# First weights in two transfers: rows 0 to 15, then rows 16 to 127

## The chip, the cores and the metric

The kernel runs on one core of a Trainium2 chip. It is one launch, and all inputs lie in the chip's memory when it starts. The metric is the device time in microseconds (us); lower is better. All data are 32-bit floats.

The core has five engines that run side by side and wait for each other by semaphores: TensorE (matmuls), VectorE, ScalarE, GpSimd, and SyncE, which computes nothing and here issues the transfers. Sixteen DMA engines move the bytes. On-chip memory has 128 rows (partitions); a transfer names a stretch of each row that it fills.

## The reference, cut to what matters

One token goes through a transformer block with adaptive layer norm. Attention has 32 heads of width 192 and a cache of 8192 positions, and an MLP with squared ReLU follows.

```
mod = silu(c) @ w_mod                        # (640) @ (640, 3840): sa, ca, ga, sb, cb, gb
h = layernorm(x) * (1 + ca) + sa
q = h @ wq                                   # (640) @ (640, 6144)
p = softmax(q . k_cache / sqrt(192))         # 32 heads x 8192 positions
x = x + ga * ((p . v_cache) @ wo)
h = layernorm(x) * (1 + cb) + sb
x = x + gb * (relu(h @ w1 + b1) ** 2 @ w2 + b2)
```

The two caches are 201 MB each. Nearly all that is moved is read once and used once.

## The kernel before, in words

**Layout and slots.** The host lays every input out so that a transfer reads one long contiguous stretch for each of the 128 rows. On chip there are three large slots, which are reused in turn (`slot`). The first holds the first weights (`wm0_t`); the chunks of the caches follow in the next ones. `PLAN` lists the chunks; each holds some key positions, some units of values, and now and then a block of `wq` or `wo`. After the chunks come three more loads: the rest of `w_mod`, then `w1`, then `w2`.

**The first weights.** `wm0` has 128 rows of 8514 floats (34,056 bytes a row, 4257 KB in all): the columns of `w_mod` for `sa` and `ca` except for a part of their last block of rows, the first block of `wq`, and x, c and the biases. One transfer brings it (L131). The rest of that last block comes as `wm0x` in six small transfers (L134), by the table `XP`. Its entries are (first row, rows, slabs): the rows of one such transfer lie four apart, as 32, 36, ..., 60 or 0, 4, 8. The place that they fill is set to zero first, half of it by VectorE (L129) and half by GpSimd (L130), so SyncE waits for these two before it issues L134.

**The order of the work at the start.** SyncE issues, in program order: the first weights (L131), the six small transfers (L134), the first and second chunk (L249, `load(0)` and `load(1)`), and the third chunk (`load(2)`) once the first slot has been used up. From then on it issues chunk n + 3 when chunk n has been used up. On the compute side VectorE copies x, c and the biases out of the first weights (L138), ScalarE and VectorE make silu(c) (L186 to L189), TensorE multiplies by the columns of `w_mod` (L207, L213), the layer norm follows (L166 to L181), then the first block of queries (L266). Only then can VectorE multiply the first keys (L285).

**The steady part.** For each chunk, VectorE multiplies keys by the query (L285) and sums each product over the width (L293), with a share of the sums done by GpSimd (L411). TensorE takes the values (L334). The order is written out by hand (`manual_schedule`), and the framework adds the semaphores: a reader waits for the transfer that fills its tile, and a transfer into a slot waits for the slot's last readers.

**The end.** The six transfers of `w2` each have a semaphore of their own. `finish` multiplies each part as it lands (L491), VectorE adds up (L499 to L502), and two small transfers write the result.

Of the kernel before, what the change touches and what calls it, by code (L numbers as in the profile page):

```python
# [13 lines left out]
P = 128  # L14
# [26 lines left out]
SX = 7  # L41
XP = ((32, 8, 5), (0, 3, SX), (1, 3, SX), (2, 3, SX), (3, 3, 6), (33, 1, SX))
WX = 3 * DG
W0 = KB * 2 * D - WX
VPC = 5
LEAD_FROM = 1300
# [54 lines left out]
def block_kernel(ctx: ExitStack, tc: tile.TileContext, kept, kv, wm0, wm0x, wm1, w1, w2):  # L101
    nc = tc.nc
# [7 lines left out]
    def slot(name):  # L110
        taken.append(name)
        return kept["slots"][(len(taken) - 1) % 3]
# [14 lines left out]
    wm0_t = slot("wm0_t")  # L127
    wm0x_t = wm0_t[:64, SLOT - SX * WX:]
    nc.vector.memset(wm0x_t[:, :SX // 2 * WX], 0.0)  # L129
    nc.gpsimd.memset(wm0x_t[:, SX // 2 * WX:], 0.0)  # L130
    nc.sync.dma_start(wm0_t[:, :wm0.shape[1]], wm0)  # L131
    r = 0
    for a, k, n in XP:
        nc.sync.dma_start(wm0x_t[a:a + 4 * k:4, :n * WX], wm0x[r:r + k, :n * WX])  # L134
        r += k

    small = const.tile([P, 2 * KB + SX + FB + KB], F32, name="small")
    nc.vector.tensor_copy(small, wm0_t[:, W0 + WQ:wm0.shape[1]])  # L138
    x_c, c_c, bbc = small[:, :KB], small[:, KB:2 * KB + SX], small[:, 2 * KB + SX:]
# [122 lines left out]
    def query(u, w):  # L262
        w = w.rearrange("p (b n) -> p b n", b=KB)
        ps = psum.tile([P, 512], F32, tag="q", name=f"ps_q{u}", bufs=2)
        for b in range(KB):
            nc.tensor.matmul(ps, h1[:, b:b + 1].to_broadcast([P, P]), w[:, b], start=(b == 0), stop=(b == KB - 1))  # L266
        nc.scalar.activation(qb[:, QC * u % RING:QC * u % RING + QC], ps, AF.Copy, scale=DH ** -0.5)  # L267
# [4 lines left out]
    nc.gpsimd.memset(att_s, 0.0)  # L272
    query(0, wm0_t[:, W0:W0 + WQ])

# [295 lines left out]
```

## Time and profile before

| | |
|---|---|
| time, median of 3 runs | 1050.31 us (1050.29 to 1050.44) |
| the profiled execution's own time | 1050.39 us |
| its span, first to last instruction | 1049.1 us |
| bytes read from the chip's memory | 451.82 MB |
| mean rate over the span | 431 GB/s |
| VectorE busy | 826.6 us (79%) |
| TensorE busy | 490.4 us (47%) |
| GpSimd busy | 190.4 us (18%) |
| ScalarE busy | 44.9 us (4%) |

Times in the trace count from the span's start. A group's line has its source line, engine, operation, tiles (written <- read) and shapes, then its count, busy time and mean length, then the idle time of the engine before it and what ended most of that. In the table of stages a packet of a transfer counts in the stage in which it starts. [...]

### The profile page before, as it was taken

What the parts mean: (1) busy time and instruction counts of PE and PEld (TensorE: products, weight loads), DVE (VectorE), ACT (ScalarE), POOL (GpSimd) and SP (SyncE); (2) the same over time, 40 slices, a digit from 0 to 9 for tenths busy, and PEclk for the clock granted to TensorE, in tenths of its full rate; (3) what the DMA queues carried; (4) which work ended last, traced back from release to release, by engine and by line L of the source; (5) the groups of instructions that cost most, each with busy time, mean ns of one, the idle gap of its engine ahead of it and who ended that gap; (6) DMA issues with size and microseconds to landing.
All of it is one profiled execution on the core that took longest, in us unless ns stands there. A gap on an engine that the chain in (4) does not pass through costs nothing.

```text
span 1049.1 us, 5218 instructions
## 1 busy us (share of the span) xinstructions
PE 490.4 (47%) x2162; PEld 136.0 (13%) x2162; DVE 826.6 (79%) x407; ACT 44.9 (4%) x122; POOL 190.4 (18%) x61
## 2 busy tenths in 40 slices
PE   3253334455352363436254366344445336436288
PEld 1010011111010010101011011011111002001023
DVE  1799878886959969888697895999887977988912
ACT  0100000000000000000000000000000000000001
POOL 1113121121212211212121121122221211311300
PEclk9676576777675686668766576676776767768689
DMA  9999999999999999999999999999999999999998
GB/s 408 431 434 433 432 433 435 437 434 436 438 437 434 431 433 431 433 433 434 432 436 435 435 435 432 433 429 435 431 438 438 434 438 434 433 435 431 421 425 364
DMA packets 9433, 452.16 MB, mean 431 GB/s; under 512 B 1065, under 2 KB 1325, under 8 KB 1709
## 3 DMA queue, kind: packets, MB, share of 16 engines
q1 hardware_dynamic: 9406, 451.83, 99.6%
q8 instruction: 17, 0.28, 0.1%
q14 instruction: 6, 0.05, 0.0%
q10 hardware_dynamic: 4, 0.00, 0.0%
HBM read 451.82 MB, written 0.00 MB: 431 GB/s over the span
## 4 chain that ended last, share of the span: by engine, by line
DMA 54%; DVE 33%; PE 12%; ACT 1%; issue 0%; SPq 0%; DVEq 0%; ACTq 0%
DMA slot<-in_kv 50%; DVE slot L285 17%; DVE sc L293 13%; PE ps_o L334 6%; DMA slot<-in_w 3%; PE ps_q L266 2%; PE att_a L366 2%; DMA slot<-in_wm 1%; DVE os L348 1%; PE ps_mx L309 1%; DVE om L346 1%; ACT p L317 0%; PE ps_mod L207 0%; PE att_a L368 0%; PE ps_mod L213 0%
## 5 line engine op out<-in xcount | busy, mean ns | idle before, releaser
L285 DVE TENSOR_TENSOR slot<-slot,qb 128x8064 f32<-128x8064 f32 (+19 forms) x81 | 419.7, 5211 | 127.0 <-DMA slot<-in_kv 121.9
L293 DVE TENSOR_REDUCE sc<-slot 128x25 f32<-128x4800 f32 (+21 forms) x109 | 333.9, 3096 | 0.4
L411 POOL TENSOR_TENSOR slot<-slot 128x1824 f32<-128x1824 f32 (+9 forms) x51 | 187.3, 3673 | 801.2 <-DVE slot L285 698.3
L334 PE MATMUL ps_o<-slot,p 128*32 128x512 f32 x1536 | 291.5, 725 | 70.4 <-DMA slot<-in_kv 60.9
L309 PE MATMUL ps_mx<-ident,mp 128*128 128x128 f32 x32 | 14.5, 452 | 347.9 <-DVE mp L307 347.9
L334 PEld LDWEIGHTS ps_o<-slot,p 128*32 128x32 f32 x1536 | 68.0, 130 | 269.8 <-issue 200.4
L366 PE MATMUL att_a<-slot,oW 128*32 128x512 f32 x96 | 64.8, 831 | 44.9 <-ACT oW L364 44.9
L266 PE MATMUL ps_q<-slot,ln_h 128*128 128x512 f32 x120 | 71.8, 759 | 26.9 <-DMA slot<-in_kv 24.7
L309 PEld LDWEIGHTS ps_mx<-ident,mp 128*128 128x128 f32 x32 | 5.6, 176 | 375.9 <-DVE mp L307 307.6
L317 ACT ACTIVATE p<-sc,nm 128x256 f32<-128x256 f32 x32 | 16.2, 507 | 650.4 <-DVE nm L311 650.4
L266 PEld LDWEIGHTS ps_q<-slot,ln_h 128*128 128x128 f32 x120 | 28.8, 251 | 67.2 <-issue 36.9
L346 DVE TENSOR_TENSOR om<-ps_o,mask 96x512 f32<-96x512 f32 x32 | 21.6, 675 | 8.9 <-PE ps_o L334 8.9
L311 DVE TENSOR_REDUCE nm<-ps_mx 128x1 f32<-128x128 f32 x32 | 9.3, 292 | 19.6 <-PE ps_mx L309 19.6
L366 PEld LDWEIGHTS att_a<-slot,oW 128*32 128x32 f32 x96 | 12.2, 142 | 81.2 <-ACT oW L364 47.6
L348 DVE TENSOR_REDUCE os<-om 96x64 f32<-96x512 f32 x32 | 21.8, 682 | 1.1
L356 DVE TENSOR_REDUCE oT<-ps_oT 128x3 f32<-128x96 f32 x16 | 4.0, 248 | 20.4 <-PE ps_oT L352 20.4
L322 PE MATMUL ps_sum<-ident,wide 128*128 128x128 f32 x16 | 7.5, 466 | 22.4 <-ACT wide L320 22.4
L352 PE MATMUL ps_oT<-ident,os 96*128 96x96 f32 x16 | 5.0, 313 | 25.4 <-DVE os L348 25.3
L207 PE MATMUL ps_mod<-slot,silu 128*32 128x480 f32 (+2 forms) x78 | 9.2, 610 | 14.4 <-DVE silu L189 14.4
L368 PE MATMUL att_a<-slot,oW 128*96 128x384 f32 x32 | 14.2, 524 | 0.0
L364 ACT ACTIVATE oW<-oT,r 128x96 f32<-128x96 f32 x16 | 5.9, 372 | 174.4 <-DVE oT L356 174.4
L267 ACT ACTIVATE qb<-ps_q 128x512 f32<-128x512 f32 x12 | 7.2, 597 | 131.9 <-PE ps_q L266 131.9
(81 smaller groups left out, 91.4 us busy)
## 6 DMA issues: line engine op xcount, KB each, us to landing
slot<-in_kv SPq DMA_DIRECT2D x38, 8064.0 KB, 35.4
slot<-in_kv SPq DMA_DIRECT2D x11, 8000.0 KB, 37.4
slot<-in_kv SPq DMA_DIRECT2D x2, 7872.0 KB
slot<-in_kv SPq DMA_DIRECT2D x1, 6144.0 KB, 22.8
slot<-in_wm SPq DMA_DIRECT2D x1, 4480.0 KB
slot<-in_wm SPq DMA_DIRECT2D x1, 4257.0 KB, 12.5
slot<-in_kv SPq DMA_DIRECT2D x1, 3264.0 KB
slot<-in_kv SPq DMA_DIRECT2D x1, 3072.0 KB
```

Source lines behind the costliest of these rows:

```text
L266: nc.tensor.matmul(ps, h1[:, b:b + 1].to_broadcast([P, P]), w[:, b], start=(b == 0), stop=(b == KB - 1))
L285: nc.vector.tensor_mul(pr, pr, q[:, None, :].to_broadcast([P, b - a, DH]))
L293: nc.vector.tensor_reduce(sc[:, a % SRING:a % SRING + b - a], src[:, a - first:b - first], axis=AX.X, op=ALU.add)
L309: nc.tensor.transpose(ps[:, :P], mp.to_broadcast([P, P]), ident)
L311: nc.vector.tensor_reduce(nm, ps[:, :P], axis=AX.X, op=ALU.max, negate=True)
L317: nc.scalar.activation(p, s[:, :, None].to_broadcast([P, NPOS, 32 // E]), AF.Exp, bias=nm, accum_out=sp[:, h % 2:h % 2 + 1])
L334: nc.tensor.matmul(ps_t[h][32 * g:32 * (g + 1)], p[:, E * j:E * (j + 1)].rearrange("p e r -> p (e r)"), t[:, g], start=(j == 0), stop=last)
L346: nc.vector.tensor_mul(om[:n], ps_t.pop(h)[:n].rearrange("p (d e) -> p d e", e=E), mask[:n, None, :].to_broadcast([n, ED, E]))
L348: nc.vector.tensor_reduce(os_[:n, h % 2], om[:n], axis=AX.X, op=ALU.add)
L366: nc.tensor.matmul(att_a[96:, :512], oW[:, j], w[:, j, :512], start=(first and j == 0), stop=(last and j == NV - 1))
L368: nc.tensor.matmul(att_a[:96, :NV * (D - 512)], oW.rearrange("p j r -> p (j r)"), w[:, :, 512:], start=first, stop=last)
L411: nc.gpsimd.tensor_add(half, half, kt[:, m:, DH // 2:])
```

## The change

The transfer of the first weights is split by rows. SyncE first issues rows 0 to 15, in full width, and then rows 16 to 127, in full width. The bytes, their source and their place are the same. The transfers of L134 and of the chunks follow in the same order as before. Readers of the first weights wait for both transfers. The split uses a new constant, 16.

```
@@ -41,6 +41,7 @@
 WX = 3 * DG
+FIRST = 16
 W0 = KB * 2 * D - WX
@@ -128,7 +129,8 @@
     nc.vector.memset(wm0x_t[:, :SX // 2 * WX], 0.0)
     nc.gpsimd.memset(wm0x_t[:, SX // 2 * WX:], 0.0)
-    nc.sync.dma_start(wm0_t[:, :wm0.shape[1]], wm0)
+    for a, b in ((0, FIRST), (FIRST, P)):
+        nc.sync.dma_start(wm0_t[a:b, :wm0.shape[1]], wm0[a:b])
     r = 0
     for a, k, n in XP:
         nc.sync.dma_start(wm0x_t[a:a + 4 * k:4, :n * WX], wm0x[r:r + k, :n * WX])
```

More of the change, by code (lines that the diff above doesn't have):

```diff
@@ L43 @@
 WX = 3 * DG
+FIRST = 16
 W0 = KB * 2 * D - WX
@@ L130, in block_kernel @@
     nc.gpsimd.memset(wm0x_t[:, SX // 2 * WX:], 0.0)
-    nc.sync.dma_start(wm0_t[:, :wm0.shape[1]], wm0)
+    for a, b in ((0, FIRST), (FIRST, P)):
+        nc.sync.dma_start(wm0_t[a:b, :wm0.shape[1]], wm0[a:b])
     r = 0
```

## The prediction

> **What bounds the kernel now.** I read the page's rows of shares and slices first, then its rows on the DMA queues, then busy time by stage.
>
> ```profile
> PE 490.4 (47%) x2162; PEld 136.0 (13%) x2162; DVE 826.6 (79%) x407; ACT 44.9 (4%) x122; POOL 190.4 (18%) x61
> DMA  9999999999999999999999999999999999999998
> DMA packets 9433, 452.16 MB, mean 431 GB/s; under 512 B 1065, under 2 KB 1325, under 8 KB 1709
> q1 hardware_dynamic: 9406, 451.83, 99.6%
> DMA 54%; DVE 33%; PE 12%; ACT 1%; issue 0%; SPq 0%; DVEq 0%; ACTq 0%
> ```
>
> No compute engine is near full: VectorE has 79% of the span, TensorE 47%. The one SyncE queue has its packets on the 16 DMA engines for 99.6% of it. The chain of waits names VectorE for a third, but the DMA queue works on meanwhile. By stage (start:end, length, busy time and count of PE, PEld, DVE, ACT and POOL, the granted clock, the DMA engines' busy share, GB/s; a packet counts where it starts):
>
> ```profile
> 0.00:13.00 13.00, 0.00 (x0) 0.00 (x0) 1.61 (x3) 1.28 (x1) 3.08 (x10) 1.00 0.93 382
> 13.00:32.00 19.00, 13.77 (x75) 6.14 (x76) 4.74 (x17) 1.76 (x3) 0.00 (x0) 0.82 1.00 433
> 51.00:1030.00 979.00, 459.96 (x1878) 121.86 (x1882) 797.54 (x366) 38.55 (x111) 184.45 (x51) 0.71 1.00 433
> 1042.00:1047.00 5.00, 4.06 (x128) 3.18 (x128) 0.35 (x2) 0.00 (x0) 0.00 (x0) 1.00 0.70 276
> 1047.00:1049.10 2.10, 0.05 (x7) 0.00 (x0) 0.60 (x3) 0.00 (x0) 0.00 (x0) 0.99 0.00 1
> ```
>
> From 13 us to 1030 us the share is 1.00 at 433 GB/s, and after the last weights only about 2 us remain. 451.83 MB at 433 GB/s are 1043.5 us, and the span is 1049.1. So the time is: when the DMA engines start, plus the bytes, plus a short tail. Whatever an engine loses in the first load it has no idle time left to win back; it comes out at the end, for the engine that is last.
>
> The change lies wholly in the first 13 us. The next views are the chain of waits there (start, length, what) and that time cut into rounds.
>
> ```profile
> 0.73 12.52 DMA slot<-in_wm
> ...
> 14.44 4.75 PE ps_mod L207 x36
> ...
> 27.84 6.57 PE ps_q L266 x10
> ...
> 35.07 12.97 DVE slot L285
> 48.06 10.22 DVE sc L293 x2
> ```
>
> ```profile
> 1.70:2.20 0.50, 0.00 (x0) 0.00 (x0) 0.27 (x1) 0.31 (x1) 0.50 (x1) 1.00 3.33 954
> 2.20:2.70 0.50, 0.00 (x0) 0.00 (x0) 0.50 (x1) 0.00 (x0) 0.50 (x1) 1.00 0.36 136
> 2.70:3.50 0.80, 0.00 (x0) 0.00 (x0) 0.49 (x1) 0.00 (x0) 0.80 (x2) 1.00 0.00 0
> 3.50:4.70 1.20, 0.00 (x0) 0.00 (x0) 0.00 (x0) 0.00 (x0) 0.18 (x1) 1.00 1.06 454
> 4.70:5.95 1.25, 0.00 (x0) 0.00 (x0) 0.00 (x0) 0.00 (x0) 0.00 (x0) 1.00 1.01 436
> ...
> 11.00:12.25 1.25, 0.00 (x0) 0.00 (x0) 0.00 (x0) 0.00 (x0) 0.00 (x0) 1.00 1.01 436
> ```
>
> One row of the first weights is 8514 floats, 34,056 bytes. 954 GB/s over 0.5 us are 477 KB, 14 rows; 136 over 0.5 are 2 more; then none starts until 3.5 us; 454 over 1.2 are 16, and 436 over 1.25 are 16 again. So the 16 engines carry a row each at a time, in eight rounds, 128 rows. A round takes 1.25 us, and 433/16 = 27.1 GB/s per engine gives the same (1.26). The first round is slower: its 14 early rows have 3.33 x 16 x 0.5 / 14 = 1.9 us each.
>
> **The change part by part.** *One issue becomes two.* The order of SyncE's issues, and what it waited for:
>
> ```profile
> 0.73 0.39 SPq L131 DMA_DIRECT2D slot<-in_wm  x1
> 3.28 4.10 SPq L134 DMA_DIRECT2D slot<-in_wm0x  x6
> 7.43 6.16 SPq L249 DMA_DIRECT2D slot<-in_kv  x2
> ```
>
> ```profile
> SPq L134 <- DVE slot L129: 2.1, 1, 2.1
> SPq L249 <- DMA slot<-in_wm: 5.5, 1, 5.5
> SPq L249 <- PE ps_q L266: 18.6, 1, 18.6
> ```
>
> The second issue costs another 0.39 us on SyncE, from about 1.13 to 1.52, inside the 2.1 us for which that queue waits for the memset of L129 anyway. Cost nothing; without that cover it would be 0.39 us on the later issues, whose bytes are still queued behind 10 us of rows. The second transfer's first row can start about 1.0 us after its issue (the first did: 0.73 to 1.7), so near 2.1 us, before any first row ends at 3.5: no gap between the two.
>
> *A wait moves.* SyncE waited 5.5 us at a chunk load for the first weights: the ninth transfer it issued waited for the first, so eight completions can be outstanding. Now the ninth is the first chunk, not the second, and it waits for the 16 rows; behind it on SyncE are all later chunk loads. SyncE is there at 7.43 us. If the 16 rows land by 4 us it waits for nothing; if at about 7.5, next to nothing, with rows of the second transfer still queued. The second chunk waits for the 112 rows as it waited for the 128. VectorE's copy of L138 needs both landings. Zero.
>
> *The start.* With fewer rows to lay out, the first row could start sooner. Bound: the whole excess of the first round, 1.9 - 1.25 = 0.65 us, gained; or nothing. No row of this trace shows how soon a transfer of fewer rows starts. I take 0, because the first 16 rows already start within about 1 us of one another.
>
> *The first round.* Before, the dealing of 128 rows gave each engine eight, and 16 engines ran at full rate together. Now the first 16 rows to be written are neighbours, rows 0 to 15. Nothing in this trace writes 16 neighbouring rows at once. Bounds: each row has a path of its own, and the round is 1.25 us as now; or all 16 share one, 16 x 1.25 = 20 us, +18.75. Between 1 and 16 I take 4 to a path, the middle in ratio, which is also the step at which the kernel's own extra transfers (L134, XP) set the rows that go at one time: 4 x 1.25 = 5.0 us in place of 1.25, +3.75 us.
>
> [...]
>
> *The other seven rounds.* 112 rows are seven to an engine. Bounds: as smooth as now, 7 x 1.25 = 8.75 us, +0; or every round shared by four as the first, 7 x 3.75 = +26.25. [...] If each engine gets seven consecutive rows, engines start seven rows apart, so mostly in different groups of four, but they drift through each other's paths. I take two to three lost rounds in all for the engine that is last, +3.0 us.
>
> [...] If only 14 engines took the 112 (eight each), the sum would be one round more, +1.25, in place of the +0. No run here shows it.
>
> *Sum.* 0 + 0 + 0 + 3.75 + 3.0 = +6.75 us. The compute that waits for the first weights (the matmuls of L207 at 14.44 and all behind them) moves by as much. That adds nothing of its own: the third chunk's load, freed by the query's matmuls at 34.41 (27.84 + 6.57), is issued while the second chunk is still coming in; 8064 KB are 19 us at 433 GB/s, and the whole queue moves with the start. VectorE has 127 us of idle before its multiplications, of which 121.9 ended by chunks landing:
>
> ```profile
> L285 DVE TENSOR_TENSOR slot<-slot,qb 128x8064 f32<-128x8064 f32 (+19 forms) x81 | 419.7, 5211 | 127.0 <-DMA slot<-in_kv 121.9
> ```
>
> The profiled execution took 1050.39 us (span 1049.1), the median of the runs is 1050.31. 1050.39 + 6.75 = 1057.14; by the median, 1057.1.
>
> **The rivals.** *No sharing that counts*: rows of neighbours are written at full rate, or the rows are dealt to the engines by place as before, so that an engine gets its rows in two transfers instead of one and the change does nothing. The sum is then 0, less up to 0.65 us: 1049.7 to 1050.4, say 1050.2. For it: 1.00 at 433 GB/s throughout, whichever rows the engines hold, and the hidden issue. Against: all those transfers have 128 rows; none shows neighbours alone. This is the case on the other side (not slower), and it decides if the first 16 rows take under some 3 us.
>
> *Sharing in the first round only*: the 112 rows then run in seven clean rounds, and the sum is +3.75: 1054.1. For it: nothing in the second transfer need put two engines on one group. [...]
>
> *Sharing in every round*: if row n goes to engine n modulo 16, each round is 16 neighbours, and the sum is 3.75 + 26.25 = +30.0: 1080.4. For it: nothing excludes it. Against: the eight smooth rounds of now show a dealing that doesn't do this with 128 rows.
>
> *A real gain*: over 0.2% is 2.1 us. The engines carry nothing before 1.7 us and lose 0.65 in the first round; to win 2.1 us they would have to start 1.4 us earlier, 0.3 us in, before SyncE's issue at 0.73. It would need a smoother stream afterwards, of which 433 GB/s leaves no sign: 1047.5.
>
> **How the numbers follow.** Forecast (sharing in the first round, partly after) 0.48; sharing in the first round only 0.08; in every round 0.06; no sharing 0.35; a real gain 0.03. A measurement of this kernel can tell about 0.2%, 2.1 us, from no change. Slower is the sum of the first three, 0.62; same 0.35; faster 0.03. The likeliest alone: 3.75 + 1.25 = +5.0 to 3.75 + 5.0 = +8.75 (four lost rounds), 1055.3 to 1059.1. The range of 8 in 10 reaches down over the no-sharing case, 1049.8, and up to 1059.6; it leaves out the case of 1080, the gain, and the edges.
>
> **What would show it.** In the rounds after the change: if 16 rows start near 2 us and the next 16 not before 6 us, the first round shared by four; if at 3.5, it didn't share. If 16 more start every 1.25 us after that, the 112 rows run clean; fewer per 1.25 us are lost rounds. The first matmul of L207 at 14.44 should move to about 21, and the last weights and the end by the same amount; from the first chunk on the stages should show 1.00 and 433 GB/s. SyncE's first extra issue should stay at 3.28. I am wrong in mechanism if the first weights land near 13.25 us; wrong in size if they land late and the end moves by less, because the late engines had slack that this trace, which doesn't tell the engines apart, hides.

## The result, and the profile after

The changed kernel takes 1059.68 us (median of 5 runs, 1059.48 to 1059.76) against 1050.33 (5 runs, 1050.29 to 1050.71): ratio 1.0088, 95% interval 1.0077 to 1.0099, so 9.35 us slower. The forecast was +6.75 us, 1057.1. The measured time lies 0.08 us above the range's upper end of 1059.6, and above the likeliest case's own 1055.3 to 1059.1.

The profiled execution's span is 1058.3 us, 9.2 more than before. From the page of the changed kernel:

```profile
span 1058.3 us, 5220 instructions
...
GB/s 258 432 439 439 429 427 432 432 439 441 431 430 432 433 435 433 441 431 426 439 437 429 432 439 433 432 435 436 432 437 434 435 432 432 429 432 445 425 424 362
...
q1 hardware_dynamic: 9422, 451.83, 99.6%
```

The bytes are the same and the queue is still busy for 99.6% of the span. But "busy" is not "moving": in the first of the 40 slices, 26.5 us long, the rate is 258 GB/s (408 in the first slice before). After that it is as before. The stages of the changed kernel (start:end, length, busy time of PE, PEld, DVE, ACT and POOL, granted clock, DMA share, GB/s) say the same:

```profile
0.00:13.00 13.00, 0.00 (x0) 0.00 (x0) 1.61 (x3) 1.28 (x1) 3.08 (x10) 1.00 0.97 204
13.00:32.00 19.00, 7.54 (x65) 3.34 (x66) 0.75 (x4) 0.21 (x1) 0.00 (x0) 1.00 0.98 343
51.00:1030.00 979.00, 452.08 (x1829) 119.13 (x1829) 804.86 (x364) 36.10 (x106) 187.37 (x51) 0.71 1.00 433
```

The share is about as high as before (0.97 and 0.98, against 0.93 and 1.00), the rate is not: each engine holds a row all the time, and the rows take longer. From 51 us to 1030 us it is 433 GB/s, as before.

The rounds show it row by row. 16 rows start in each of these windows of the changed kernel, and in the three windows with a rate of 0 none starts. In a window with 16 rows, share times length is the mean time of one row.

```profile
1.70:2.20 0.50, 0.00 (x0) 0.00 (x0) 0.27 (x1) 0.31 (x1) 0.50 (x1) 1.00 7.55 1090
2.20:5.00 2.80, 0.00 (x0) 0.00 (x0) 0.98 (x1) 0.00 (x0) 1.48 (x2) 1.00 0.00 0
5.00:6.10 1.10, 0.00 (x0) 0.00 (x0) 0.00 (x0) 0.00 (x0) 0.00 (x0) 1.00 2.67 495
6.10:8.10 2.00, 0.00 (x0) 0.00 (x0) 0.00 (x0) 0.00 (x0) 0.00 (x0) 1.00 0.00 0
8.10:8.80 0.70, 0.00 (x0) 0.00 (x0) 0.00 (x0) 0.00 (x0) 0.00 (x0) 1.00 3.40 778
8.80:10.60 1.80, 0.00 (x0) 0.00 (x0) 0.00 (x0) 0.00 (x0) 0.00 (x0) 1.00 0.00 0
10.60:11.20 0.60, 0.00 (x0) 0.00 (x0) 0.00 (x0) 0.00 (x0) 0.00 (x0) 1.00 3.23 908
12.60:13.50 0.90, 0.00 (x0) 0.00 (x0) 0.00 (x0) 0.00 (x0) 0.00 (x0) 1.00 2.08 605
14.40:15.30 0.90, 0.00 (x0) 0.00 (x0) 0.00 (x0) 0.00 (x0) 0.00 (x0) 1.00 2.39 605
16.40:17.70 1.30, 0.00 (x0) 0.00 (x0) 0.00 (x0) 0.00 (x0) 0.00 (x0) 1.00 1.82 419
18.80:20.00 1.20, 0.00 (x0) 0.00 (x0) 0.00 (x0) 0.00 (x0) 0.00 (x0) 1.00 1.85 454
```

The rows take 3.8 us in the first round (7.55 x 0.5), then 2.9, 2.4, 1.9, 1.9, 2.2, 2.4 and 2.2, against 1.25 before. The sixteen engines stay nearly in step: the 16 rows of a round start within 1.3 us of one another.

The chain of waits shows the weights complete at 23.20 us (1.17 + 22.03) in place of 13.25, and the first matmul at 24.46 in place of 14.44:

```profile
1.17 22.03 DMA slot<-in_wm
...
24.46 4.23 PE ps_mod L209 x36
```

That is +10.0 us for the last of the first weights. What goes on to the end is slightly less: in the trace the last row's own record ends at 22.20 us in place of 12.89, +9.3 us, and the landing follows it by 1.0 us in place of 0.4. The first chunk's load (6144 KB; columns are count, KB, us from issue to landing) went from

```profile
slot<-in_kv SPq DMA_DIRECT2D x1, 6144.0 KB, 22.8
```

before to

```profile
slot<-in_kv SPq DMA_DIRECT2D x1, 6144.0 KB, 32.1
```

after. With the issue at 7.43 and now 7.46 us, that is +9.3 us, and the span ends 9.2 us later. From the first chunk on the whole loss is simply carried.

SyncE's part came out as the prediction had it:

```profile
0.73 0.84 SPq L133 DMA_DIRECT2D slot<-in_wm  x2
3.28 4.13 SPq L136 DMA_DIRECT2D slot<-in_wm0x  x6
7.46 16.11 SPq L251 DMA_DIRECT2D slot<-in_kv  x2
...
SPq L251 <- DMA slot<-in_wm: 15.4, 1, 15.4
```

The second issue fits ahead of 3.28 us. The first chunk is issued as early as before. The wait of 15.4 us at the second chunk lies behind a queue that is full (the first chunk is in it until 32.1 us after its issue).

### The profile page after: what moved, and what is told of

It reads as the page before. It is cut to its first block, busy times and chain, and to the rows that moved or that the text cites. A ratio compares the mean times of both kernels' runs of the same rounds, so it can differ in the third digit from the quotient of the medians.

```text
span 1058.3 us, 5220 instructions
## 1 busy us (share of the span) xinstructions
PE 489.1 (46%) x2162; PEld 135.0 (13%) x2162; DVE 826.6 (78%) x407; ACT 44.9 (4%) x122; POOL 190.4 (18%) x61
## 3 DMA queue, kind: packets, MB, share of 16 engines
q1 hardware_dynamic: 9422, 451.83, 99.6%
## 4 chain that ended last, share of the span: by engine, by line
DMA 57%; DVE 33%; PE 9%; ACT 1%; issue 0%; SPq 0%; DVEq 0%; ACTq 0%
DMA slot<-in_kv 52%; DVE slot L287 17%; DVE sc L295 13%; PE ps_o L336 5%; DMA slot<-in_w 3%; DMA slot<-in_wm 2%; PE ps_q L268 1%; PE att_a L368 1%; DVE os L350 1%; DVE om L348 1%; PE ps_mx L311 1%; ACT p L319 1%; PE ps_mod L209 0%; PE ps_mod L215 0%; DVE nm L313 0%
## 5 line engine op out<-in xcount | busy, mean ns | idle before, releaser
L354 PE MATMUL ps_oT<-ident,os 96*128 96x96 f32 x16 | 5.0, 313 | 25.6 <-DVE os L350 25.4
## 6 DMA issues: line engine op xcount, KB each, us to landing
slot<-in_kv SPq DMA_DIRECT2D x1, 6144.0 KB, 32.1
```

## The experiments

Theory ("paths"), an assumption of the author's that the times below test and that no trace shows directly: there are 16 write paths, as many as the engines that write 128 rows at 433 GB/s together, each about as fast as one engine (27.1 GB/s). In a transfer of all 128 rows each engine has a path of its own (1.25 us a row). Neighbouring rows, by fours, and the four rows 32 further on, share one, so a transfer of neighbouring rows has its engines wait for each other (2.68 us a row in e2, 3.85 in e5). Rivals: that the split as such costs (a second issue, a moved wait, a count other than 128); that the 16 rows ahead push the engines out of step and the 112 suffer from it; other paths, such as eight consecutive rows to one, or each four rows with one of their own.

Eight kernels, all made from the kernel before:

| run | first weights | median us | change us | ratio, 95% interval |
|---|---|---|---|---|
| e1 | cut by columns | 1050.42 | +0.06 | 1.000 (0.9991 to 1.001) |
| e2 | cut by rows at 64 | 1061.12 | +10.8 | 1.0102 (1.0084 to 1.0120) |
| e3 | extra 128 rows ahead | 1060.36 | +10.0 | 1.0095 (1.0079 to 1.0111) |
| e4 | extra rows 16 to 127 ahead | 1065.34 | +15.0 | 1.0143 (1.0127 to 1.0159) |
| e5 | extra rows 0 to 15 ahead | 1054.54 | +4.24 | 1.0041 (1.0026 to 1.0056) |
| e6 | extra 16 rows, four apart | 1052.75 | +2.45 | 1.0023 (1.0013 to 1.0032) |
| e7 | extra 16 rows, eight apart | 1052.76 | +2.46 | 1.0023 (1.0013 to 1.0032) |
| e8 | eight transfers of 16 rows | 1077.72 | +27.4 | 1.0258 (1.0243 to 1.0273) |

The kernel before took 1050.36 beside e1 to e4 and 1050.30 beside e5 to e8.

**e1, two transfers of 128 rows.**

```
-    nc.sync.dma_start(wm0_t[:, :wm0.shape[1]], wm0)
+    for a, b in ((0, 1064), (1064, wm0.shape[1])):
+        nc.sync.dma_start(wm0_t[:, a:b], wm0[:, a:b])
```

> The first weights in two transfers of all 128 rows, cut by columns (the first 1064 of 8514, then the rest). Paths theory (neighbouring rows share a write path, so what counts is which rows a transfer holds): +0, within 0.3 us of before, first weights landed near 13.3 us. Two-transfers theory (the second issue, the moved wait of SyncE, or any split costs): +9 us like the change, or a good part of it.

Measured: +0.06 us. Two transfers, with the second issue and the moved wait, cost nothing that can be measured. The weights are complete at 13.5 us (13.25 before). The first of the two carries 532 KB, as the 16 rows do.

**e2, two transfers of 64 rows.**

```
+    for a, b in ((0, 64), (64, P)):
+        nc.sync.dma_start(wm0_t[a:b, :wm0.shape[1]], wm0[a:b])
```

> Cut by rows at 64 in place of 16. Paths theory with 16 paths of eight rows, of which 64 neighbouring rows reach eight: two engines to each path in every round, 8 x 2.5 us = 20 us in place of 10, so +10 us, with 16 rows starting every 2.5 us. If only four neighbours share and each group has a path of its own: every engine has its own four rows, +0. If rows were dealt n modulo 16: every round 5 us, +30. If it is the count of rows being other than 128 that costs, in the odd shares of seven: 64 is four to an engine, so +0 to +2.

Measured: +10.8 us, against +10 for two engines to a path; some 0.35 us of it is a later start, as no row starts before 2.05 us. Windows of this kernel, of four of its rounds, 16 rows in each:

```profile
6.70:7.70 1.00, 0.00 (x0) 0.00 (x0) 0.00 (x0) 0.00 (x0) 0.00 (x0) 1.00 2.68 545
9.40:10.40 1.00, 0.00 (x0) 0.00 (x0) 0.00 (x0) 0.00 (x0) 0.00 (x0) 1.00 2.68 545
12.00:13.05 1.05, 0.00 (x0) 0.00 (x0) 0.00 (x0) 0.00 (x0) 0.00 (x0) 1.00 2.38 519
...
17.20:18.20 1.00, 0.00 (x0) 0.00 (x0) 0.00 (x0) 0.00 (x0) 0.00 (x0) 1.00 2.68 545
```

A row takes 2.68 us (2.68 x 1.00), and rounds follow each other by 2.7 us. That is a factor of two, a little more than 2 x 1.25. The window at 12.00 has the first rows of the second half, which go to other paths by the theory: they take 2.5 us (2.38 x 1.05). An odd share of rows isn't needed: four rows to an engine are slow too. It also excludes a dealing by n modulo 16, which asked for +30.

**e3 and e4, the 112 rows by themselves.** In both an extra transfer goes ahead of an untouched load of the first weights.

```
+    nc.sync.dma_start(kept["slots"][2][:, :wm0.shape[1]], wm0)            # e3
+    nc.sync.dma_start(kept["slots"][2][16:, :wm0.shape[1]], wm0[16:])     # e4
     nc.sync.dma_start(wm0_t[:, :wm0.shape[1]], wm0)
```

> Before, with one extra transfer ahead of all: all 128 rows of the first weights once more, into the slot that the second chunk fills later; it is read by nobody. It is 4257 KB more: eight rounds of 1.26 us, +10.1 us by every theory. The yardstick for the run with 112 rows.

> The same extra transfer with rows 16 to 127 alone, 112 rows, 3725 KB; it is read by nobody. By bytes: seven rounds of 1.26 us, +8.8 us, less than with 128 rows. Paths theory: seven rounds of about 2.2 us as in the change, +13 to +16 us, more than with 128 rows though it moves fewer bytes. If the slow rounds of the change were an after-effect of the 16 rows ahead (engines pushed out of step), +9 to +10.

Measured: +10.0 and +15.0 us. Sixteen rows fewer take 5 us more. There is nothing ahead of the 112 rows here, so the slow rounds aren't an after-effect. In e4, the first window reaches to the end of the 112 rows, the second over most of the 128:

```profile
1.70:18.30 16.60, 0.00 (x0) 0.00 (x0) 1.26 (x1) 0.31 (x1) 1.98 (x2) 1.00 1.01 261
18.30:27.20 8.90, 0.00 (x0) 0.00 (x0) 0.00 (x0) 0.00 (x0) 0.00 (x0) 1.00 1.01 432
```

A row counts where it starts, and 15 of the 128 start in the first window; the 112 alone are 230 GB/s over its 16.6 us (112 x 34,056 bytes). The full rate is back as soon as the 128 rows flow. The price of seven rounds is 15.0 us, 2.14 us each.

**e5, e6 and e7, sixteen rows at three spacings.**

```
+    nc.sync.dma_start(kept["slots"][2][:16, :wm0.shape[1]], wm0[:16])         # e5
+    nc.sync.dma_start(kept["slots"][2][0:64:4, :wm0.shape[1]], wm0[:16])      # e6
+    nc.sync.dma_start(kept["slots"][2][0:128:8, :wm0.shape[1]], wm0[:16])     # e7
     nc.sync.dma_start(wm0_t[:, :wm0.shape[1]], wm0)
```

> Before, with one extra transfer ahead of all: rows 0 to 15 of the first weights once more, into rows 0 to 15 of the slot that the second chunk fills later; it is read by nobody. One row to an engine. By bytes: +1.26 us. Paths theory: four rows to a path, +5.0 us (4 x 1.26). If eight consecutive rows made a path: +10.

> The same extra bytes, written to rows 0, 4, ..., 60 of that slot; read by nobody. Paths theory as the halves left it, with rows 32 apart on one path (16 paths of two groups of four, eight paths in each half): two rows to a path, +2.5 us. If each group of four had a path of its own: +1.26. If eight consecutive rows made a path: +2.5.

> The same extra bytes, written to rows 0, 8, ..., 120 of that slot; read by nobody. Paths theory with rows 32 apart on one path: rows 0, 32 share, 8 and 40, and so on, two to a path, +2.5 us. If eight consecutive rows made a path, or each group of four its own: one row to a path, +1.26.

Measured: +4.24, +2.45 and +2.46 us, for the same bytes from the same source rows. So it is the place written to that counts. Not all of the +2.45 is sharing, though. SyncE takes longer to issue the spread rows, in e5 and then in e6:

```profile
0.73 0.38 SPq L131 DMA_DIRECT2D slot<-in_wm  x1
```

```profile
0.73 0.64 SPq L131 DMA_DIRECT2D slot<-in_wm  x1
```

The first rows start some 0.4 us later in e6 and e7: none starts from 1.70 to 2.10 us, where all 16 of e5 do. That leaves about 2.05 us, between the 1.26 of one row to a path and the 2.5 of two, so part of the agreement with +2.5 is luck.

e6 and e7 together leave one picture of those tried: with eight consecutive rows to a path e7 would have cost 1.26, or 1.7 with the later start, and with a path for each group of four both would. Rows 32 apart sharing gives 2.5 for both. So would rows 16 apart, which no run was made to tell apart. The rows' own times say the same as the totals. The 16 rows start in this window, in e5 and then in e6:

```profile
1.70:3.00 1.30, 0.00 (x0) 0.00 (x0) 1.07 (x1) 0.31 (x1) 1.30 (x1) 1.00 2.96 419
```

```profile
1.70:3.00 1.30, 0.00 (x0) 0.00 (x0) 1.07 (x1) 0.31 (x1) 1.30 (x1) 1.00 1.62 419
```

That is 3.85 us a row in e5 (2.96 x 1.30) and 2.11 in e6, where the first 16 rows before took 1.85. The 16 rows behind them are slowed too, to 2.4 us in e5 and 1.7 in e6 in place of 1.26. And so do the landings. For 532 KB, from issue to landing, in e1 (all 128 rows), e7, e6 and e5:

```profile
slot<-in_wm SPq DMA_DIRECT2D x1, 532.0 KB, 3.9
```

```profile
slot<-in_wm SPq DMA_DIRECT2D x1, 532.1 KB, 5.0
```

```profile
slot<-in_wm SPq DMA_DIRECT2D x1, 532.1 KB, 5.1
```

```profile
slot<-in_wm SPq DMA_DIRECT2D x1, 532.1 KB, 7.0
```

By the theory that is one, two, two and four rows to a path, with the later start of 0.4 us in the two in the middle. e5 missed its number: 4.24, not 5.0.

**e8, nothing but neighbours.**

```
+    for a in range(0, P, 16):
+        nc.sync.dma_start(wm0_t[a:a + 16, :wm0.shape[1]], wm0[a:a + 16])
```

> The first weights in eight transfers of 16 neighbouring rows, nothing added. Paths theory with the engines kept in step, as the rounds of the changed kernel show them: every round has four rows to a path, 8 x 5.0 us = 40 us in place of 10, +30 us. If engines can run ahead into the next transfer, whose rows lie on four other paths: between +10 and +30. If only the odd share of seven rows were at fault: +0 to +3, for eight more issues.

Measured: +27.4 us, near the +30 of engines that stay in step. The profiled execution took 1076.29 us, +26.0, which is what its rounds give (8 x 4.52 - 10.0 = 26.2); why the other three took 1.4 us more isn't shown. Two of its rounds, five apart:

```profile
9.10:10.90 1.80, 0.00 (x0) 0.00 (x0) 0.00 (x0) 0.00 (x0) 0.00 (x0) 1.00 2.54 303
...
31.70:33.50 1.80, 0.00 (x0) 0.00 (x0) 0.00 (x0) 0.00 (x0) 0.00 (x0) 1.00 2.54 303
```

16 rows start each time, 22.6 us apart over five rounds: 4.52 us a round, 2.54 x 1.8 = 4.6 us a row. Four to a path cost 3.6 times one row, not four times. By the theory the next transfer's rows lie on other paths. All 16 engines end their rows within 1.8 us of one another, so they run ahead by no more than that. SyncE's waits don't add to this: it was held up for the small transfers (22.2 us in six waits) and the chunks (8.4 in two), but in the trace the engines have rows all the while, 4.6 us a row in rounds of 4.52 us.

**The sum closes.** The 16 rows cost 4.24 us by themselves (e5), the 112 cost 15.0 (e4), and the 128 that they replace cost 10.0 (e3): 4.24 + 15.0 - 10.0 = +9.2 us, against the +9.35 measured for the change.

## Why the prediction was right or wrong, point by point

**What bounds the kernel: right.** The loss of the first load, +9.3 us at the first chunk, arrives undiminished at the end (+9.2). The last row of the first weights ends 9.3 us later as well, so no slack of late engines shows.

**One issue becomes two, a wait moves: right, 0.** e1 has both and costs 0.06 us.

**The start: right, 0.** The first rows start in the window 1.70 to 2.20 us before and after.

**The first round: right in mechanism, somewhat large.** +3.75 us was put down, from four rows to a path. The four was taken as the middle between 1 and 16, with the step of the kernel's own small transfers as a hint and no time in the trace before behind it; as far as that trace goes it was luck. A round of four to a path takes 4.52 us and not 5.0 (e8), and by itself it costs 4.24 (e5), of which a clean row would be 1.25: +3.0 us. In the trace of the change the first rows seem to end sooner, after 3.8 us, but the transfer lands 6.6 us after its issue:

```profile
slot<-in_wm SPq DMA_DIRECT2D x1, 532.1 KB, 6.6
```

That is 7.3 us, when the second round's rows have all started (by 6.1). So a part of the first round's price stands in the second round's longer rows. The landing by about 7.5 us that the prediction gave for sharing was right; its test by the start of the second round (not before 6 us) was too strict.

As to which rows share, four neighbours and the four rows 32 further on fit the runs: +10.8 us against +10 (e2), +2.45 and +2.46 against +2.5 (e6, e7). A share with the four rows 16 further on would fit e2 and e5 to e7 too. It would have every second transfer of e8 stay on the paths of the one before, and e8's rounds are all alike (4.5 to 4.6 us a row), which speaks against it, though weakly. The 545 KB of a round of e8 in 4.52 us are 121 GB/s, but in transfers that overlap by up to 1.8 us on different paths, by the theory.

**The other seven rounds: the step that failed, in size.** "I take two to three lost rounds in all for the engine that is last, +3.0 us." Alone, the seven rounds take 15.0 us in place of 8.75, +6.2: five lost rounds. Sixteen rows start in each round of the change, so all sixteen engines take part, and the case of 14 engines is out.

The reckoning was of one engine that now and then meets another, with the others running free. The windows show all sixteen slow, and nearly in step: in the last six rounds the mean row takes 1.9 to 2.4 us, and no row in the trace under 1.78. The assumed seven consecutive rows to an engine don't give that by themselves. Counted by the theory, with the engines in step, two or four of the sixteen would be on a shared path in each round, and the mean row would take an estimated (4 x 2.68 + 12 x 1.25) / 16 = 1.6 us at most. So either the rows are dealt in another order, in which most engines share by twos, or something holds back the engines that share nothing. No run tells these apart, and the cause of the larger loss stays open; in e2 and e8 every engine shares alike by the theory, so their even rounds don't decide it. Seven full rounds of two to a path would be 7 x 2.68 = 18.8 us; it was 15.0, so not every engine shares all the time. The modulo dealing is out, at 7 x 4.52 = 31.6 us for the 112 rows.

With +3.0 and +6.2 for the two rounds' terms the sum would have been +9.2.

**The rivals.** No sharing is out by e5 to e7. Sharing in the first round only, +3.75, is out by e4: most of the loss lies in the other seven. Sharing by four in every round is what e8 does, +27.4, not the change. The likeliest case's low end puts down 1.25 us for the other seven rounds; no run shows that term, and the 112 rows alone took 15.0 us in place of 8.75 (e4), +6.2.

## What to carry to other kernels

On a queue that is always full, as this one, where a transfer's rows lay on chip counted before its bytes: 112 rows took 15.0 us where 128 took 10.0, and the same 16 rows took 4.24 or 2.45 us by their place. To bring something earlier, cut by columns, with all 128 rows in each piece (+0.06 us here), and not by rows (+9.35 at 16, +10.8 at 64). And a busy DMA share said only that engines held work (0.97 at 204 GB/s in the first 13 us of the change, 0.93 at 382 before); read the GB/s beside it.

## What the runs showed that was not expected

Where by the theory all engines share alike, rounds follow each other evenly: every 2.7 us for two to a path (e2) and every 4.52 us for four (e8), with the 16 starts of a round within 1.0 and 1.8 us. Two to a path cost slightly more than twice a clean row (2.68 against 2 x 1.25): by the theory a path moves 25.4 GB/s with two writers (2 x 34,056 bytes in 2.68 us), where one engine alone moves 27.1. Four cost less than four times (4.52 against 5.0). That isn't the rate of one path with four writers, because in e8 the first engines start on the next transfer's rows, by the theory on other paths, up to 1.8 us before the last end the old ones; the one round of e2 at which, by the theory, the paths change is shorter too (2.5 us against 2.68). Whether this overlap is the whole difference stays open.
